# Reordering the start of a fused attention and gated FFN kernel, and its passage from batch 0 to batch 1

## The chip, the cores and the metric

The kernel runs on one core of one Trainium2 chip. The metric is the time of one execution on the device in microseconds (us). Executions of one and the same kernel differ by up to about 1 us here, so differences of a few tenths are read from the traces, one profiled run for each kernel, and the times are used as a check.

## The reference

The inputs are q, k and v of 8 batches, 8 heads, 576 positions and 64 elements, and three FFN weights, all in f32.

```python
q_s = exp(q - max(q, -1));  q_s /= sum(q_s, -1)        # softmax over the 64 elements of a head
k_s = exp(k - max(k, 2));   k_s /= sum(k_s, 2)         # softmax over the 576 positions
kv  = einsum('bhsd,bhse->bhde', k_s, v)
x   = einsum('bhsd,bhde->bhse', q_s, kv)               # 4608 tokens of 512 elements
g   = x @ w_gate                                       # 512 x 1536
out = (gelu(g) * (x @ w_val)) @ w_out                  # 1536 x 512
```

## The kernel before

For each batch the kernel takes exps of q and k (ScalarE), sums and norms (VectorE, partly GpSimd), casts v to f16, transposes q on TensorE ("unit_t"), forms kv for two heads at a time ("hp", four pairs in a batch), masks and scales it into `kv_sb`, multiplies to x ("unit_x") and casts x to f16. The FFN follows: `psg` and `psv` are the gate and value products, `psy` the output product. Every engine runs its instructions in the order in which the program emits them.

The start ("head" below: all that comes before the large matmuls of batch 0 run without a break), with cuts:

```python
def ksum_mm(hps):                       # column sums of exp(k), one PSUM tile for all four pairs
    ...
def kv0_mm(hp):                         # kv of two heads: 128x128, of which the mask keeps two 64x64 blocks
    pool, tag = (ps_att, "att") if hp == 0 else (ps_big, "mm")
    st[("pskv0", hp)] = pool.tile([P, P], f32, name="pskv0", tag=tag)
    for n in range(NC):                 # NC = 5 chunks of positions
        nc.tensor.matmul(st[("pskv0", hp)], ek_b[0][:, n, hp * P:(hp + 1) * P],
                         v16_b[0][:, n, 2 * hp:2 * hp + 2, 0:D], start=(n == 0), stop=(n == NC - 1))
def kv0_norm(hp):                       # VectorE: kv_sb = pskv0 * 1/sum * mask
    ...
def unit_t(b, g, eng="dve"):            # 8 transposes into one bank, then one copy to eqt
    ...
def unit_x(b, hp, eng="act", big=False):
    nc.tensor.matmul(psx, st[(b, "kv", hp)].rearrange("p h e -> p (h e)"), xq(b, hp), start=True, stop=True)
    copy_on(eng, xt[:, hp, :], psx)
...
evac_t0("dve")
warm_pe(2); ksum_mm((0, 1)); warm_pe(2); ksum_mm((2, 3))
cast_v(0, 0, 2, "dve")                  # heads 0 and 1 of v
cast_v(0, 2, 4, "act")
ksum_rec()
cast_v(0, 4, 6, "act")
kv0_mm(0); kv0_mm(1); kv0_norm(0); kv0_norm(1)
cast_v(0, 6, 8, "dve")
...                                     # loads of the next batches; first casts of the weights on GpSimd
unit_x(0, 0, "act", True)
kv0_mm(2)
unit_x(0, 1, "act", True)
kv0_norm(2)
unit_t(0, 1, "dve")
```

Work of the next batch rides between the matmul groups of the present one; `at(batch, kind, place, ...)` registers it. For the passage from batch 0 to batch 1:

```python
at(0, NS, 16, L(unit_kv, 1, 0), L(cast_v, 1, 4, 8), L(load_batch, 2, ((v, "v"),)))
at(0, NS, 6, L(norm, 1, 3))
at(0, NS, 17, L(unit_x, 1, 0, "act", True), L(unit_x, 1, 1, "act", True))
first1 = ([[L(unit_kv, 1, 1), L(unit_t, 1, 1)], [], [L(unit_x, 1, 3, "dve")]],
          [[], [], [L(unit_x, 1, 2, "act")]])
...
cut = 10 if ns == 3 else NFI            # where in the last output group of batch 0 the riders go
```

Much later, among the last FFN groups of batch 1:

```python
at(1, FI, 6, L(norm, 2, 3))             # batch 2's last norm: VectorE sums, reciprocal, multiply
at(1, FI, 10, L(unit_t, 2, 1))          # its transposes on TensorE
at(1, FI, 11, ..., L(cast_v, 3, 0, H))  # batch 3's v, four casts on GpSimd
```

The softmax here doesn't subtract the row's maximum and nothing guards it: scores larger than these inputs give would overflow.

## Time and profile before

| | before |
|---|---|
| time, 3 runs | 315.99 us median (315.94 to 316.39) |
| span of the profiled run | 314.5 us |
| k landed, v landed (start of ScalarE's first exp of k and first cast of v) | 10.02, 12.62 us |
| first large matmul (`psg`) | 15.41 us |
| its third block (ninth large matmul: x of batch 0 is complete) | 17.85 us |
| the same third block of batch 1 | 53.13 us |

Timeline lines are to be read as: start (us), duration (us), engine, source line, operation, output<-inputs, shapes, count, and in brackets the idle time ahead of the instruction with the engine that ended it. A matmul of 512 columns is shown as 0.38 us long, but the next one can start 0.216 us after it, so successive starts are what tells the pace. The prediction shows the lines of before.

### The profile page before, as it was taken

How to read it: one execution, taken by the hardware profiler on the slowest of the kernel's cores; microseconds unless marked ns; L12 is line 12 of the kernel's file. 1: busy time of each engine (PE TensorE's matmuls, PEld its weight loads, DVE VectorE, ACT ScalarE, POOL GpSimd, SP SyncE). 2: the span in 40 equal slices, each digit the busy share in tenths (PEclk: the TensorE clock that was granted, in tenths of full speed). 3: DMA queues.
4: the chain of work that ended last, by engine and by line, in shares of the span. 5: the costliest groups of instructions: out<-in, count | busy, mean ns of one | idle time of the engine just before them, and what ended most of it. 6: DMA issues, size and time to landing. Idle time of an engine off the chain costs nothing.

```text
span 314.5 us, 4799 instructions
## 1 busy us (share of the span) xinstructions
PE 307.7 (98%) x1826; PEld 143.7 (46%) x1826; DVE 191.1 (61%) x324; ACT 138.5 (44%) x178; POOL 44.7 (14%) x59
## 2 busy tenths in 40 slices
PE   8899999999999999999999999999999999999995
PEld 3444454444444444444444444444444444444443
DVE  3844386597898479746984599458943434324331
ACT  3753564988433663356334643374330233013300
POOL 2657451331001200030003000300000000000000
PEclk9999999999999999999999999999999999999999
DMA  7999999950178116921492139303021200140002
GB/s 231 372 383 394 401 386 388 395 194 0 69 245 306 53 70 194 349 59 67 127 386 80 72 90 383 115 27 131 1 58 28 115 18 0 35 101 0 3 33 100
DMA packets 42343, 50.78 MB, mean 161 GB/s; under 512 B 3408, under 2 KB 38096, under 8 KB 42320
## 3 DMA queue, kind: packets, MB, share of 16 engines
q1 hardware_dynamic: 40592, 48.84, 45.0%
q10 hardware_dynamic: 1728, 1.64, 1.6%
q8 instruction: 14, 0.23, 0.3%
q14 instruction: 9, 0.07, 0.1%
HBM read 37.75 MB, written 9.44 MB: 150 GB/s over the span
## 4 chain that ended last, share of the span: by engine, by line
PE 90%; DVE 4%; DMA 2%; ACT 2%; issue 1%; ACTq 0%; DVEq 0%
PE psy L489 29%; PE psg L411 28%; PE psv L411 27%; DMA qt<-in_q_dram 2%; PE pskv L284 1%; DVE eq L200 1%; PE psl L510 1%; PE psx L383 1%; DVE rq L191 1%; DVE rq L181 1%; DVE ht L418 1%; PE psx L365 1%; ACT eq L163 1%; PE pst L306 1%; ACT L416 0%
## 5 line engine op out<-in xcount | busy, mean ns | idle before, releaser
L416 ACT ACTIVATE gl<-psg 128x512 f32<-128x512 f32 x108 | 64.0, 599 | 131.0 <-PE psg L411 124.5
L418 DVE SCALAR_TENSOR_TENSOR ht<-psv,gl 128x512 f16<-128x512 f32 x108 | 72.9, 682 | 64.6 <-PE psv L411 64.1
L411 PE MATMUL psg<-xt,wg_sb 128*128 128x512 f16 x384 | 100.5, 379 | 0.1
L411 PE MATMUL psv<-xt,wv_sb 128*128 128x512 f16 x384 | 100.5, 379 | 0.0
L489 PE MATMUL psy<-wo_sb,ht 128*128 128x512 f16 x420 | 94.0, 379 | 0.0
L411 PEld LDWEIGHTS <-wv_sb 128*128 128x128 f16 x432 | 42.3, 98 | 51.2 <-issue 0.8
L411 PEld LDWEIGHTS <-wg_sb 128*128 128x128 f16 x432 | 41.9, 98 | 49.4 <-issue 0.4
L489 PEld LDWEIGHTS <-ht 128*128 128x128 f16 x420 | 40.4, 98 | 47.9 <-issue 0.8
L538 DVE TENSOR_SCALAR yo<-psy 128x512 f32<-128x512 f32 x30 | 20.5, 685 | 29.7 <-PE psy L489 29.7
L139 POOL CAST v<-vt 128x640 f16<-128x640 f32 x26 | 18.8, 763 | 137.1 <-DMA vt<-in_v_dram 98.3
L181 DVE TENSOR_REDUCE rq<-eq 128x10 f32<-128x640 f16 x28 | 22.7, 812 | 6.1 <-ACT eq L163 5.7
L200 DVE TENSOR_TENSOR eq<-eq,rrq 128x640 f16<-128x640 f16 (+1 forms) x29 | 23.7, 817 | 0.3
L163 ACT ACTIVATE ek<-kt 128x1280 f16<-128x1280 f32 (+1 forms) x11 | 19.1, 1746 | 3.4 <-DMA kt<-in_k_dram 3.3
L163 ACT ACTIVATE eq<-qt 128x2560 f16<-128x2560 f32 (+2 forms) x10 | 18.4, 1863 | 2.3 <-DMA qt<-in_q_dram 2.2
L331 DVE STREAM_TRANSPOSE et<-eq 128x640 f16<-128x640 f16 x20 | 16.9, 845 | 0.7
L411 PE MATMUL psg<-xtr,wg_sb 128*128 128x512 f16 x48 | 12.3, 379 | 0.0
L411 PE MATMUL psv<-xtr,wv_sb 128*128 128x512 f16 x48 | 12.3, 379 | 0.0
L143 DVE CAST xt<-psx 128x512 f16<-128x512 f32 x16 | 10.2, 682 | 1.2 <-PE psx L365 1.2
L403 PE MATMUL pswarm<-warm,ident 128*128 128x512 f16 x34 | 9.5, 438 | 1.4 <-POOL ident masks.py:199 1.4
L163 ACT ACT_TABLE_LOAD x8 | 10.3, 1283 | 0.6 <-DMA qt<-in_q_dram 0.5
L141 ACT CAST xt<-psx 128x512 f16<-128x512 f32 x16 | 8.7, 588 | 3.5 <-PE psx L365 3.5
L141 ACT CAST xtr<-psxr 128x128 f16<-128x128 f32 (+1 forms) x6 | 1.7, 283 | 17.8 <-PE psxr L383 17.8
(74 smaller groups left out, 122.6 us busy)
## 6 DMA issues: line engine op xcount, KB each, us to landing
out_dram<-yo SPq DMA_DIRECT2D x14, 512.0 KB, 3.5
kt<-in_k_dram SPq DMA_DIRECT2D x7, 640.0 KB, 7.9
vt<-in_v_dram SPq DMA_DIRECT2D x7, 640.0 KB, 8.4
qt<-in_q_dram SPq DMA_DIRECT2D x7, 640.0 KB, 6.5
qt<-in_q_dram SPq DMA_DIRECT2D x8, 512.0 KB, 6.7
eqt<-et SPq DMA_DIRECT2D x80, 40.0 KB, 1.9
wost<-in_moe_w_out_dram SPq DMA_DIRECT2D x6, 512.0 KB, 7.9
kt<-in_k_dram SPq DMA_DIRECT2D x6, 512.0 KB, 8.1
```

Of the source, the lines that this page charges most:

```text
L139: nc.gpsimd.tensor_copy(out=dst, in_=src)
L141: nc.scalar.copy(out=dst, in_=src)
L143: nc.vector.tensor_copy(out=dst, in_=src)
L163: nc.scalar.activation(out=dst[:, n0:NC, h0 * D:h1 * D].rearrange(o, d=D, **({"t": 2} if b >= QUAD else {})), in_=heads(tiles[(nm, b)], b, ...
L181: nc.vector.reduce_sum(rq, e, axis=mybir.AxisListType.X)
L200: (nc.gpsimd if eng == "pool" else nc.vector).tensor_tensor(out=e, in0=e, in1=rrq.unsqueeze(-1).to_broadcast((P, n, 2, D)), op=ALU.mult)
L331: nc.vector.transpose(out=et[:, :, hp].rearrange("p c (n i) -> p n c i", i=32), in_=eq_b[b % 2][:, :, hp * P:(hp + 1) * P].rearrange("p n ...
L411: nc.tensor.matmul(ps, w[:, ci, fi * P:(fi + 1) * P], xt[:, ci, :], start=(ci == 0), stop=(ci == HP - 1))
L416: nc.scalar.activation(out=gl, in_=psg, func=ACTF.Gelu)
L418: nc.vector.scalar_tensor_tensor(out=ht, in0=psv, scalar=_H_SCALE, in1=gl, op0=ALU.mult, op1=ALU.mult)
L489: nc.tensor.matmul(psy, hts[fi][:, ns * P:(ns + 1) * P], wo_sb[:, fi, :], start=(fi == 0), stop=(fi == NFI - 1))
L538: nc.vector.tensor_scalar(out=yo, in0=psy, scalar1=1.0 / _H_SCALE, scalar2=None, op0=ALU.mult)
```

## The change

The intent is to start the large matmuls sooner and to close the gaps at the passage. In the head, kv of batch 0 is computed on column halves (20 matmuls of 64 columns instead of 10 of 128 for two pairs), v is cast head by head on two engines, the first x is split over two banks and cast by ScalarE and VectorE at once, and the second group of transposes is spread between these steps. At the passage, kv, norm and x of batch 1 move up within batch 0. The diff, cut to its core:

```diff
     def kv0_mm(hp):
-        pool, tag = (ps_att, "att") if hp == 0 else (ps_big, "mm")
-        st[("pskv0", hp)] = pool.tile([P, P], f32, name="pskv0", tag=tag)
+        ps = ps_big.tile([P, D], f32, name="pskv0", tag="mm")
         for n in range(NC):
-            nc.tensor.matmul(st[("pskv0", hp)], ek_b[0][:, n, hp * P:(hp + 1) * P],
-                v16_b[0][:, n, 2 * hp:2 * hp + 2, 0:D], start=(n == 0), stop=(n == NC - 1))
+            for s in range(2):
+                c0 = hp * P + s * D
+                nc.tensor.matmul(ps[s * D:(s + 1) * D], ek_b[0][:, n, c0:c0 + D],
+                                 v16_b[0][:, n, 2 * hp + s, 0:D], start=(n == 0), stop=(n == NC - 1))
 ...  (ksum_mm and ksum_rec work on two pairs at a time; unit_t takes a list of functions to run between its halves)
+    def unit_x_halves(b, hp):
+        for i, eng in enumerate(("act", "dve")):
+            c = slice(i * MAIN // 2, (i + 1) * MAIN // 2)
+            psx = ps_big.tile([P, MAIN // 2], f32, name="psx", tag="mm")
+            nc.tensor.matmul(psx, ..., xq(b, hp)[:, c], start=True, stop=True)
+            copy_on(eng, get_xt(b)[:, hp, c], psx)
 ...
-    warm_pe(2); ksum_mm((0, 1)); warm_pe(2); ksum_mm((2, 3))
-    cast_v(0, 0, 2, "dve"); cast_v(0, 2, 4, "act"); ksum_rec(); cast_v(0, 4, 6, "act")
-    kv0_mm(0); kv0_mm(1); kv0_norm(0); kv0_norm(1)
+    warm_pe(2); ksum_mm(0); ksum_rec(0); ksum_mm(1)
+    cast_v(0, 0, 1, "dve"); cast_v(0, 1, 2, "act"); cast_v(0, 2, 3, "dve"); cast_v(0, 3, 4, "act")
+    cast_v(0, 4, 6, "act")
+    unit_t(0, 1, None, (lambda: kv0_mm(0), lambda: kv0_norm(0), lambda: kv0_mm(1),
+                        lambda: kv0_norm(1), lambda: unit_x_halves(0, 0)))
+    evac_t1 = st["evac_t"]
+    unit_x(0, 1, "act", True)
+    kv0_mm(2)
+    evac_t1("dve")
+    ksum_rec(1)
+    kv0_norm(2)
     cast_v(0, 6, 8, "dve")
 ...
-    unit_x(0, 0, "act", True); kv0_mm(2); unit_x(0, 1, "act", True); kv0_norm(2); unit_t(0, 1, "dve")
 ...
-    at(0, NS, 16, L(unit_kv, 1, 0), L(cast_v, 1, 4, 8), L(load_batch, 2, ((v, "v"),)))
-    at(0, NS, 6, L(norm, 1, 3))
+    at(0, NS, 16, L(unit_kv, 1, 0), L(cast_v, 1, 4, 8), L(load_batch, 2, ((v, "v"),)),
+       L(norm, 1, 3))
-    first1 = ([[L(unit_kv, 1, 1), L(unit_t, 1, 1)], [], [L(unit_x, 1, 3, "dve")]],
-              [[], [], [L(unit_x, 1, 2, "act")]])
+    first1 = [[L(unit_t, 1, 1), L(unit_kv, 1, 1)], [L(unit_x, 1, 2, "act")],
+              [L(unit_x, 1, 3, "dve")]]
-                cut = 10 if ns == 3 else NFI
+                cut = 9 if ns == 2 else 7 if ns == 3 else NFI
```

More of the change, by code (lines that the diff above doesn't have):

```diff
@@ L236, in kv_norm @@
         for j in range(2):
-            kv_sb = att.tile([P, 2, D], f16, name="kv_sb", tag="kv", bufs=12)
+            kv_sb = att.tile([P, 2, D], f16, name="kv_sb", tag="kv", bufs=8)
             nc.vector.scalar_tensor_tensor(
@@ L242, in kv_norm, with ksum_mm, ksum_rec @@
             st[(b, "kv", 2 * g + j)] = kv_sb
-    def ksum_mm(hps):
-        if "pks" not in st:
-            st["pks"] = ps_big.tile([P, HP], f32, name="pks", tag="mm")
-        for hp in hps:
+    def ksum_mm(g):
+        st[("pks", g)] = ps_big.tile([P, 2], f32, name="pks", tag="mm")
+        for j in range(2):
+            hp = 2 * g + j
             for n in range(NC):
-                nc.tensor.matmul(st["pks"][:, hp:hp + 1], ek_b[0][:, n, hp * P:(hp + 1) * P], ones,
-                                 start=(n == 0), stop=(n == NC - 1))
-    def ksum_rec():
-        st["rck0"] = att.tile([P, HP], f32, name="rck0", tag="rck0", bufs=1)
-        nc.vector.reciprocal(out=st["rck0"], in_=st["pks"])
+                nc.tensor.matmul(st[("pks", g)][:, j:j + 1], ek_b[0][:, n, hp * P:(hp + 1) * P],
+                                 ones, start=(n == 0), stop=(n == NC - 1))
+    def ksum_rec(g):
+        st[("rck0", g)] = att.tile([P, 2], f32, name="rck0", tag="rck0")
+        nc.vector.reciprocal(out=st[("rck0", g)], in_=st[("pks", g)])
     def kv0_mm(hp):
-        pool, tag = (ps_att, "att") if hp == 0 else (ps_big, "mm")
-        st[("pskv0", hp)] = pool.tile([P, P], f32, name="pskv0", tag=tag)
+        ps = ps_big.tile([P, D], f32, name="pskv0", tag="mm")
+        st[("pskv0", hp)] = ps
         for n in range(NC):
-            nc.tensor.matmul(
-                st[("pskv0", hp)], ek_b[0][:, n, hp * P:(hp + 1) * P],
-                v16_b[0][:, n, 2 * hp:2 * hp + 2, 0:D], start=(n == 0), stop=(n == NC - 1))
+            for s in range(2):
+                c0 = hp * P + s * D
+                nc.tensor.matmul(ps[s * D:(s + 1) * D], ek_b[0][:, n, c0:c0 + D],
+                                 v16_b[0][:, n, 2 * hp + s, 0:D], start=(n == 0), stop=(n == NC - 1))
     def kv0_norm(hp):
-        kv_sb = att.tile([P, 2, D], f16, name="kv_sb", tag="kv", bufs=12)
+        kv_sb = att.tile([P, 2, D], f16, name="kv_sb", tag="kv", bufs=8)
         nc.vector.scalar_tensor_tensor(
-            out=kv_sb, in0=st[("pskv0", hp)].rearrange("p (h e) -> p h e", e=D),
-            scalar=st["rck0"][:, hp:hp + 1], in1=mask, op0=ALU.mult, op1=ALU.mult)
+            out=kv_sb, in0=st[("pskv0", hp)].unsqueeze(1).to_broadcast((P, 2, D)),
+            scalar=st[("rck0", hp // 2)][:, hp % 2:hp % 2 + 1], in1=mask, op0=ALU.mult, op1=ALU.mult)
         st[(0, "kv", hp)] = kv_sb
@@ L298, in get_eqt, with unit_t @@
         return st[(b, "eqt")]
-    def unit_t(b, g, eng="dve"):
+    def unit_t(b, g, eng="dve", between=()):
         eqt = get_eqt(b)
         pst = ps_att.tile([P, 2, MAIN], f16, name="pst", tag="att")
+        st["evac_t"] = lambda eng: copy_on(eng, eqt[:, 2 * g:2 * g + 2, 0:MAIN], pst)
         for j in range(2):
             hp = 2 * g + j
+            for f in between if j == 1 else ():
+                f()
             for n in range(NM):
@@ L308, in unit_t @@
                     eq_b[b % 2][:, n + 1, hp * P:(hp + 1) * P], ident)
-        st["evac_t"] = lambda eng: copy_on(eng, eqt[:, 2 * g:2 * g + 2, 0:MAIN], pst)
         if eng:
@@ L367, in unit_x @@
         copy_on(eng, xt[:, hp, :], psx)
+    def unit_x_halves(b, hp):
+        for i, eng in enumerate(("act", "dve")):
+            c = slice(i * MAIN // 2, (i + 1) * MAIN // 2)
+            psx = ps_big.tile([P, MAIN // 2], f32, name="psx", tag="mm")
+            nc.tensor.matmul(psx, st[(b, "kv", hp)].rearrange("p h e -> p (h e)"),
+                             xq(b, hp)[:, c], start=True, stop=True)
+            copy_on(eng, get_xt(b)[:, hp, c], psx)
     def unit_xrem(b, eng="act"):
@@ L427, in ffn_fi, with ffn_first @@
         return gate(psg, psv)
-    def ffn_first(xt, after, between):
+    def ffn_first(xt, after):
         ps = []
@@ L440, in ffn_first @@
                 mm_gv(psg, wg_sb, xt, fi, range(0, 2))
-                for f in between[fi]:
-                    f()
                 mm_gv(psv, wv_sb, xt, fi, range(0, 2))
@@ L571 @@
     warm_pe(2)
-    ksum_mm((0, 1))
-    warm_pe(2)
-    ksum_mm((2, 3))
-    cast_v(0, 0, 2, "dve")
-    cast_v(0, 2, 4, "act")
-    ksum_rec()
-    cast_v(0, 4, 6, "act")
-    kv0_mm(0)
-    kv0_mm(1)
-    kv0_norm(0)
-    kv0_norm(1)
+    ksum_mm(0)
+    ksum_rec(0)
+    ksum_mm(1)
+    cast_v(0, 0, 1, "dve")
+    cast_v(0, 1, 2, "act")
+    cast_v(0, 2, 3, "dve")
+    cast_v(0, 3, 4, "act")
+    cast_v(0, 4, 6, "act")
+    unit_t(0, 1, None, (lambda: kv0_mm(0), lambda: kv0_norm(0), lambda: kv0_mm(1),
[6 more added lines that the diff above has]
+    kv0_norm(2)
     cast_v(0, 6, 8, "dve")
@@ L590 @@
     cast_w("wv", 0, "pool")
-    unit_x(0, 0, "act", True)
-    kv0_mm(2)
-    unit_x(0, 1, "act", True)
-    kv0_norm(2)
-    unit_t(0, 1, "dve")
     preload(ACTF.Gelu)
@@ L670 @@
         if b < 2:
-            hts = ffn_first0(xt, (x_upper0, L(unit_x, 0, 3, "act"))) if b == 0 else ffn_first(xt, *first1)
+            hts = ffn_first0(xt, (x_upper0, L(unit_x, 0, 3, "act"))) if b == 0 else ffn_first(xt, first1)
             fi0 = len(hts)
```

## The prediction

> **What bounds the kernel now.** I read the page first, for which engine fills the span, then the chain of waits, then the timeline of the head (0 to 20 us) and of the passage from batch 0 to batch 1 (44 to 54 us), because the change touches only these two places.
>
> ```profile
> PE 307.7 (98%) x1826; PEld 143.7 (46%) x1826; DVE 191.1 (61%) x324; ACT 138.5 (44%) x178; POOL 44.7 (14%) x59
> PE 90%; DVE 4%; DMA 2%; ACT 2%; issue 1%; ACTq 0%; DVEq 0%
> ```
>
> The first line is busy time by engine, the second the chain that ended last by engine. TensorE (PE) is busy for 98% of the span and is 90% of the chain. The large matmuls (psg, psv, psy) start 0.216 us apart from 15.41 us to the end, and the change removes none of them. So time can only be won where the PE stream starts late or has a gap. A list of the matmul starts with more than the usual distance between them shows what there is: the start itself at 15.41 us, and three gaps at the passage, of 0.184, 0.058 and 0.189 us beyond the usual distance, 0.43 us in all. The head, in the timeline of PE (start, duration, instruction, wait before):
>
> ```profile
> 13.36 0.72 PE L261 MATMUL pskv<-v,ek 128*128 128x128 f16 x10 [0.45 <-DVE v L143]
> 14.24 0.39 PE L365 MATMUL psx<-eqt,kv_sb 128*128 128x512 f16 x1 [0.17 <-DVE kv_sb L267]
> 14.96 0.61 PE L306 MATMUL pst<-ident,eq 128*128 128x128 f16 x8
> 15.41 0.38 PE L411 MATMUL psg<-xt,wg_sb 128*128 128x512 f16 x1
> ```
>
> Here PE waits for the cast of v, then for kv, and does 8 transposes (0.45 us of issue) after x, before the first large matmul. Those are the waits that the change attacks. VectorE (DVE) at the same time:
>
> ```profile
> 14.38 0.73 DVE L143 CAST v<-vt 128x640 f16<-128x640 f32 x1
> 15.04 0.33 DVE L267 SCALAR_TENSOR_TENSOR kv_sb<-pskv,rck,mask 128x128 f16<-128x128 f32 x1
> 15.61 0.69 DVE L143 COPY eqt<-pst 128x1024 f16<-128x1024 f16 x1 [0.24 <-PE pst L306]
> ```
>
> The reader is to see that the last cast of v (heads 6 and 7) is done at 15.11 us, before the eqt copy, and that PE's fourth kv unit, which needs it, comes at 16.27 us without a wait. The passage:
>
> ```profile
> 48.23 0.59 PE L489 MATMUL psy<-wo_sb,ht 128*128 128x512 f16 x2
> 48.84 0.38 PE L411 MATMUL psg<-xt,wg_sb 128*128 128x512 f16 x1
> 49.06 0.38 PE L411 MATMUL psv<-xt,wv_sb 128*128 128x512 f16 x1
> 49.33 0.38 PE L411 MATMUL psg<-xt,wg_sb 128*128 128x512 f16 x1
> ...
> 52.73 0.38 PE L365 MATMUL psx<-eqt,kv_sb 128*128 128x512 f16 x1
> 53.13 0.38 PE L411 MATMUL psg<-xt,wg_sb 128*128 128x512 f16 x1
> ```
>
> Each jump above 0.216 us here is a wait for ScalarE's cast of an x block (0.59 us each).
>
> **What the Trainium skill says.** "TensorE: Matmul & The Clock Gate", section "Wait — 56ns, not 53.3ns?", gives warm start-to-start distances of 55.6 and 215.7 ns for 128 and 512 columns; the trace agrees (55 to 56 and 216 ns). "TensorEngine Tiling (Array Packing)", section "Key Properties": "Changing tiling mode (not just tile) drains the TensorE". The trace shows such a drain: batch 2's kv units already run on column halves, and the first of these starts 0.309 us after a 512-column matmul (0.093 too late), while the next large matmul starts 0.129 us after the last of them (about 0.11 too late). "ScalarE: Activation LUTs", section "What ACT_TABLE_LOAD costs", puts an ACTIVATE at 186 ns + 0.833 ns an element and says that successive ones overlap by about 93 ns; the trace agrees (casts of 640 and 1280 elements: 726 and 1262 ns, starts 632 ns apart). So a cast of 320 elements is estimated at 0.455 us. "PSUM — Partial Sum Buffer", section "PSUM bank collisions raise a hardware error", has two engines reading the same bank at once as a collision, which is why x in halves for two engines needs two banks; no run of before shows it.
>
> **The change in the head, step by step** (all times after are estimates).
> 1. v by heads. VectorE is free at 12.64 (the eqt copy ends). Reciprocal first: 0.17 us long, but VectorE starts the next instruction some 0.08 before the last one ends (13.31 end of cast, 13.23 next start), so head 0 starts at 12.72. Half of a 0.67 to 0.73 us cast is about 0.37, so it ends at 13.09. ScalarE starts at 12.62 (v landed) and ends head 1 at 13.08. PE may start kv at 13.14 instead of 13.36.
> 2. kv on halves: 10 matmuls in 5 pairs; in batch 2 the pairs start about 0.03 us apart, so the fifth starts 0.15 after the first and ends 0.196 later: 13.49, where the 5 whole ones took 0.44. kv_sb 0 runs from 13.52 to 13.87 (0.35 each). Heads 2 and 3 are ready at about 13.44, so kv 1 runs 13.49 to 13.84, kv_sb 1 13.88 to 14.23.
> 3. x 0 in halves: kv_sb 0 plus 0.06 gives 13.93 and 14.04 us; each half takes 0.11 + 0.17, so they end at 14.21 and 14.32. ScalarE's half cast (186 - 26 + 0.833 x 256, about 0.37) ends at 14.62, VectorE's (0.68 less 256 columns at 0.96 a ns, 0.415) at 14.78.
> 4. PE meanwhile: 4 transposes (0.22) to 14.37 (the other 4 filled the wait before kv), x 1 (0.216) to 14.59, kv 2 with both drains to 14.96. First large matmul at about 14.96: **0.45 earlier** than 15.41. The next pair needs x 1 cast by ScalarE (14.79 to 15.38), so runs from 15.43 to 15.86.
> 5. The price. The order of VectorE's instructions in the built program is now: half of x 0, eqt copy, reciprocal, kv_sb 2, **then** the cast of heads 6 and 7. From the half's start at 14.36, with starts 0.34, 0.67, 0.09 and 0.27 apart: 14.70, 15.37, 15.46, 15.73. The cast takes 0.73 and ends at about 16.43. PE needs it for kv 3 at 15.95, and its order is fixed: it waits until about 16.48. Before, kv 3 began at 16.276. What follows (kv 3, x 2, two psg, x 3, two psv) takes 1.574 us in the old trace and 0.15 + 0.13 + 6 x 0.216 = 1.575 in the new, because the 0.13 us that column halves save is what the drain costs. So the head ends **about 0.2 us later** than before, although it starts 0.45 earlier.
>
> **The change at the passage.** kv of batch 1 moves up by three matmuls (0.65 us): PE start 45.71 instead of 46.35. By the old distances (x may start 1.39 and 1.66 us after kv) x 0 may start at 47.15 and x 1 at 47.37, where PE arrives at 47.13 and 47.35, so 0.02 to 0.03 is lost. Five psy matmuls now lie between x and the first large matmul, instead of two: they cover the casts, and the gaps of 0.184 and 0.058 go. The fourth norm (0.81 + 0.22 + 0.83) comes before the output's eviction and ends at about 49.1, so the transposes at 49.5 can go ahead of kv. x 2 moves a pair of matmuls earlier, so its cast ends about 0.2 us before it is needed and the gap of 0.189 goes; x 2 itself may wait 0.03 for kv_sb. Sum: 0.43 less 0.05, **about 0.38 us won**. Fewer buffers for kv_sb (8 for 12) cost nothing, as just 8 are ever taken.
>
> **Sum:** 315.99 + 0.2 - 0.38 = 315.8. Everything from 54 us on is the same program; its two later waits (0.25 and 0.30 us, at 62.8 and 70.8 us) hang on ScalarE's exps, which start when the gelus of the same batch are done and so shift along.
>
> **Rivals.** (a) The head keeps its 0.45 us, if VectorE gets to heads 6 and 7 sooner than I reckon (short casts, more overlap). For it: VectorE's durations for 320 and 256 elements are only my scaling. Against it: the copies of eqt and of heads 6 and 7 alone are 1.3 us after 14.36. Then 315.3. It would still be capped: the last wo chunk is cast on GpSimd by 42.67, at a time that the loads set, and PE takes it at 42.88, so more than 0.2 us of head gain turns into a wait for it. (b) VectorE is slower than reckoned, or the GpSimd casts slow it, and kv 3 starts at 16.7: then the head loses 0.4 and the passage just balances it: 316.0. (c) The two warm-up matmuls that are dropped let the clock gate close and PE runs at half speed for some us. Against it: the page of before grants full clock in all slices with idle stretches of 0.5 and 0.6 us, and the new longest is about 0.7 us (11.8 to 12.5). That would be 317 or more; I give it 2%. (d) The passage's gaps are replaced by a wait for kv_sb or the fourth norm: at most 0.3 given back: 316.1.
>
> **Range and chances.** The prize is at most 0.45 + 0.43 = 0.9 us of 316, under 0.3%; a change of 2% would take 6.3 us. The three runs of before spread over 0.45 us. So I predict 315.8 us with a range of 315.2 (rival a) to 316.4 (rivals b and d, with the spread), faster 1%, within 2% 98%, slower 1%.
>
> **What would show it.** In the profile after: the first psg matmul at 14.9 to 15.0; a PE wait of about 0.5 us for VectorE's v ahead of the fourth kv unit, starting near 16.5; psg's third block (17.85 before) at 18.0 to 18.1; no gap over 0.1 us on PE between 46 and 54 us apart from drains; the last large matmuls some 0.2 us earlier than before. Wrong would be: no wait ahead of kv 3 (step 5 fails, rival a), a wait for wo's cast near 42.9, a granted clock below 1 near 13 us, or new gaps near 47 or 51 us.

## The result

The changed kernel is correct and takes 316.03 us median (four runs: 316.28, 316.24, 315.82, 315.72), against 316.15 us for four runs of before (315.94 to 316.39). The ratio of the times is 0.9995, with a 95% interval of 0.9978 to 1.0013: the same. A ratio here is the mean time of one kernel's fast runs over that of the other's of the same rounds, so it is not quite the ratio of the medians quoted. The page of the profile after, with the same two lines that the prediction shows of before:

```profile
PE 307.0 (98%) x1845; PEld 143.4 (46%) x1845; DVE 192.0 (61%) x327; ACT 138.5 (44%) x179; POOL 44.5 (14%) x59
...
PEclk9999999999999999999999999999999999999999
...
PE 89%; DVE 5%; DMA 2%; ACT 2%; issue 1%; ACTq 0%; DVEq 0%
```

TensorE is still the bound, and the clock row holds 9 throughout (mean granted clock 1.0), so the two dropped warm-up matmuls did not bring any throttling. VectorE's share of the chain grew from 4 to 5%. The timeline of TensorE in the head after:

```profile
13.10 0.74 PE L263 MATMUL pskv<-v,ek 128*64 128x64 f16 x20
13.89 0.39 PE L377 MATMUL psx<-eqt,kv_sb 128*128 128x256 f16 x2
14.12 0.39 PE L310 MATMUL pst<-ident,eq 128*128 128x128 f16 x4
14.35 0.38 PE L368 MATMUL psx<-eqt,kv_sb 128*128 128x512 f16 x1
14.65 0.35 PE L263 MATMUL pskv<-v,ek 128*64 128x64 f16 x10
14.93 0.39 PE L423 MATMUL psg<-xt,wg_sb 128*128 128x512 f16 x1
...
16.57 0.35 PE L263 MATMUL pskv<-v,ek 128*64 128x64 f16 x10 [0.58 <-DVE v L143]
...
18.16 0.38 PE L423 MATMUL psg<-xt,wg_sb 128*128 128x512 f16 x1
```

The first large matmul starts at 14.93 us instead of 15.41, but a wait for VectorE's cast of v now stands ahead of the fourth kv unit: it starts 0.74 us later than the usual distance would have it, of which the bracket shows the 0.58 in which the array was empty. The third block comes at 18.16 us (17.85 before). The timeline of VectorE after shows why:

```profile
14.32 0.42 DVE L143 CAST xt<-psx 128x256 f16<-128x256 f32 x1
14.66 0.68 DVE L143 COPY eqt<-pst 128x1024 f16<-128x1024 f16 x1
15.26 0.16 DVE L255 RECIPROCAL rck<-pks 128x2 f32<-128x2 f32 x1
15.53 0.35 DVE L268 SCALAR_TENSOR_TENSOR kv_sb<-pskv,rck,mask 128x128 f16<-128x128 f32 x1
15.79 0.73 DVE L143 CAST v<-vt 128x640 f16<-128x640 f32 x1
```

The cast of heads 6 and 7 (last line) stands behind four other instructions and ends at 16.52 us; before, it ended at 15.11. At the passage, TensorE after:

```profile
47.46 0.60 PE L368 MATMUL psx<-eqt,kv_sb 128*128 128x512 f16 x2
47.90 1.24 PE L499 MATMUL psy<-wo_sb,ht 128*128 128x512 f16 x5
48.97 0.38 PE L423 MATMUL psg<-xt,wg_sb 128*128 128x512 f16 x1
49.19 0.38 PE L423 MATMUL psv<-xt,wv_sb 128*128 128x512 f16 x1
...
52.80 0.38 PE L368 MATMUL psx<-eqt,kv_sb 128*128 128x512 f16 x1
53.02 0.38 PE L423 MATMUL psg<-xt,wg_sb 128*128 128x512 f16 x1
```

Five `psy` matmuls now cover the casts of x, and no gap over 0.03 us beyond the usual distance is left: those of 0.184, 0.058 and 0.189 us are gone.

### Counting from the landing of v

Loads do not arrive at the same time in each run: in the traces with unchanged load rates, ScalarE's first exp of k starts between 9.91 and 10.21 us, and its first cast of v between 12.54 and 12.92. In the profiled run of after v landed 0.07 us earlier than in that of before, which is no work of the change. I therefore count the landmarks from the start of ScalarE's first cast of v (us):

| run | v landed | first psg | third block | 33rd large matmul | batch 1's third block | after batch 2's transposes (241st) | last large matmul |
|---|---|---|---|---|---|---|---|
| before | 12.615 | 2.795 | 5.233 | 10.413 | 40.516 | 60.472 | 298.042 |
| after | 12.541 | 2.393 | 5.617 | 10.801 | 40.477 | 60.574 | 298.146 |
| passage alone | 12.630 | 2.800 | 5.237 | 10.417 | 40.093 | 60.039 | 297.607 |
| head alone | 12.752 | 2.393 | 5.613 | 10.793 | 40.896 | 60.751 | 298.321 |
| after, heads 6/7 on GpSimd | 12.751 | 2.393 | 4.964 | 10.792 | 40.468 | 60.568 | 298.138 |
| after, gate in an existing tile | 12.582 | 2.395 | 5.617 | 11.003 | 40.678 | 60.329 | 297.898 |
| both of these | 12.714 | 2.396 | 4.967 | 10.812 | 40.487 | 60.138 | 297.709 |
| passage alone, gate | 12.923 | 2.795 | 5.232 | 10.412 | 40.088 | 59.735 | 297.305 |

Counted so, different runs of the same stretch of program agree within about 0.01 us up to the third block, and from the 241st large matmul to the last all of them take 237.57 us. (The 33rd can differ more: 11.003 and 10.801 in two kernels that are the same up to there, which experiment 9 explains.) So everything happens in the first 61 us, and the table reads as a sum: the head costs 5.617 - 5.233 = **0.38 us**, the passage wins (40.477 - 10.801) - (40.516 - 10.413) = **-0.43 us**, together -0.04 us at 53 us. Then, up to the 241st matmul, another 0.14 us is lost, where the program has not changed at all.

### Where the last 0.14 us goes

Between 68 and 72 us VectorE multiplies batch 2's last norm while GpSimd casts batch 3's v. The timeline of VectorE before, then of GpSimd and of TensorE before:

```profile
69.85 1.23 DVE L200 TENSOR_TENSOR eq<-eq,rrq 128x640 f16<-128x640 f16 x1
```

```profile
68.34 3.31 POOL L139 CAST v<-vt 128x640 f16<-128x640 f32 x4 [7.45 <-DMA vt<-in_v_dram]
```

```profile
70.61 0.92 PE L306 MATMUL pst<-ident,eq 128*128 128x128 f16 x8
```

Here the profile merges the eight transposes into one row; 0.30 us of it is the wait for the multiply ahead of the fifth.

And after, VectorE, GpSimd and then TensorE, which waits for the multiply:

```profile
69.73 1.37 DVE L200 TENSOR_TENSOR eq<-eq,rrq 128x640 f16<-128x640 f16 x1
```

```profile
68.37 3.31 POOL L139 CAST v<-vt 128x640 f16<-128x640 f32 x4 [7.54 <-DMA vt<-in_v_dram]
```

```profile
70.50 0.39 PE L310 MATMUL pst<-ident,eq 128*128 128x128 f16 x4
71.15 0.40 PE L310 MATMUL pst<-ident,eq 128*128 128x128 f16 x4 [0.27 <-DVE eq L200]
```

The norm's multiply ahead of this one, of the same shape, takes 0.83 us where GpSimd is idle (67.29 us in the same trace). The four casts start 0.67 us apart; the third began at 69.70 us, 25 ns ahead of the multiply at 69.73. The multiply ends 0.67 us after that cast, and the fourth cast's record is stretched from 0.72 to 1.31 us. This agrees with the Trainium skill, "SBUF — State Buffer", section "Who interferes with whom": a VectorE instruction with two SBUF inputs contends with a GpSimd instruction that reads SBUF, and the one that comes later is blocked for the whole of the other. The casts start when batch 3's v has landed, not when TensorE gets there (68.34 and 68.37 us). So the multiply came 0.12 us earlier and still ended 0.03 us later; TensorE's wait for it grew from 0.30 to 0.44 us.

### The profile page after: what moved, and what is told of

Same layout as the page of the kernel before. It is cut to its first block, busy times and chain, and to the rows that moved or that the text cites. A ratio compares the mean times of both kernels' runs of the same rounds, so it can differ in the third digit from the quotient of the medians.

```text
span 314.5 us, 4843 instructions
## 1 busy us (share of the span) xinstructions
PE 307.0 (98%) x1845; PEld 143.4 (46%) x1845; DVE 192.0 (61%) x327; ACT 138.5 (44%) x179; POOL 44.5 (14%) x59
## 4 chain that ended last, share of the span: by engine, by line
PE 89%; DVE 5%; DMA 2%; ACT 2%; issue 1%; ACTq 0%; DVEq 0%
PE psy L499 29%; PE psg L423 28%; PE psv L423 27%; DMA qt<-in_q_dram 2%; PE pskv L285 1%; DVE eq L200 1%; PE psl L520 1%; PE psx L395 1%; DVE rq L191 1%; DVE rq L181 1%; DVE ht L430 1%; ACT eq L163 1%; PE psx L368 0%; PE pst L310 0%; ACT L428 0%
## 5 line engine op out<-in xcount | busy, mean ns | idle before, releaser
L143 DVE CAST xt<-psx 128x512 f16<-128x512 f32 (+1 forms) x17 | 10.7, 667 | 1.4 <-PE psx L368 1.3
L415 PE MATMUL pswarm<-warm,ident 128*128 128x512 f16 x32 | 8.7, 436 | 1.4 <-POOL ident masks.py:199 1.4
L141 ACT CAST xt<-psx 128x512 f16<-128x512 f32 (+1 forms) x16 | 8.6, 575 | 3.3 <-PE psx L368 3.0
```

The costliest lines, as they stand in the source:

```text
L141: nc.scalar.copy(out=dst, in_=src)
L143: nc.vector.tensor_copy(out=dst, in_=src)
```

## The experiments

Twelve kernels ran, all correct. They went in three calls, each with nine runs of before on the same chip (medians 316.10, 316.36 and 316.38 us).

### 1. The passage alone

Before, with the lines of the passage (`at`, `first1`, `cut`, `ffn_first`) taken from the change; the head is the old one.

> The kernel before with only the passage of the change (batch 1's kv, norm and x moved up); the head is the old one. Theory (pinned): PE is about 0.42 us earlier than before when it comes out of the passage (third block of batch 1's first psg at 52.7 instead of 53.13), but the wait ahead of batch 2's second transposes near 70.7 us grows from 0.30 to about 0.70, because VectorE's last norm multiply of batch 2 overlaps GpSimd's casts of batch 3's v, whose start is set by the load and not by PE. So from 72 us on nothing is won: span within 0.1 us of before. Rival (parts cancel: the head loses what the passage wins): no such growth, the end is 0.4 us earlier than before.

Measured: 315.83 us median (315.48 to 315.91), ratio 0.9987 (0.9975 to 1.0). In the table the passage wins 0.42 us by batch 1's third block (40.093 for 40.516), and all of it arrives at the end (297.607 for 298.042 is 0.43). The pinned theory is refuted. The multiply at 69.44 us fell upon the second cast instead of the third and was 1.22 us long, so the wait stayed at 0.29 us. The passage's gain is real and is not pinned later on. What the collision returns depends on where in a cast the multiply falls.

### 2. The head alone

The changed kernel with the passage put back as it was.

> The changed kernel with the passage put back; only the head of the change. Theory (pinned): the first large matmul near 14.94, a wait of 0.74 us ahead of the fourth kv unit, third block near 18.16, so 0.31 us later than before; the passage keeps its gaps of about 0.43, so it comes out 0.3 later than before (53.4); the wait near 70.7 shrinks from 0.30 to about 0, which takes up the loss: span within 0.1 us of before. Rival (parts cancel): the loss of 0.3 us stays to the end, span 0.3 us longer.

Measured: 316.50 us median (316.42 to 316.68), ratio 1.0012 (0.9998 to 1.0026). All five runs lie above the median of before (316.10), though the interval still touches 1. The trace is clear: third block at 5.613 for 5.233, the loss of 0.38 us again, with the 0.74 us wait for the cast of heads 6 and 7. By batch 1's third block the loss is still 0.38 (40.896 for 40.516). This time the multiply fell late in a cast (1.12 us) and the wait was 0.19 us, so 0.28 us arrive at the end. The two parts of the change cancel.

### 3 and 4. A gate ahead of GpSimd's casts

To take the collision away, GpSimd is to start batch 3's v only when the multiply is done. A 128x1 copy that reads the multiply's result does that; it writes into a new tile of 32 bytes. Once in the changed kernel:

```diff
     ones = const.tile([P, 1], f16)
+    hold = const.tile([P, 1], f16)
 ...
-       ... L(exp_rem0), L(cast_v, 3, 0, H))
+       ... L(exp_rem0),
+       lambda: nc.gpsimd.tensor_copy(out=hold, in_=eq_b[0][:, 0, 3 * P:3 * P + 1]), L(cast_v, 3, 0, H))
```

> The changed kernel, with one 128x1 copy on GpSimd that reads batch 2's last normalised block, ahead of GpSimd's casts of batch 3's v: the casts can then not overlap that norm multiply. Theory (pinned): the multiply takes 0.83 instead of 1.37 us, the wait of 0.43 ahead of the transposes near 70.7 goes, and the end is 0.43 us earlier than in the changed kernel (span about 0.4 us shorter, time ratio about 0.9987). Rival (the multiply is long for another reason, or the wait is for something else): no change beyond 0.05 us, or a longer one as the casts come later.

and once in before (there with 8 kv_sb buffers for 12, to make room for the tile):

> The kernel before with the same gate on GpSimd (and 8 buffers for kv_sb in place of 12, of which 8 are ever used, to make room). Theory (pinned): multiply 0.83 instead of 1.23 us, the wait of 0.30 near 70.7 goes, and the end is 0.3 us earlier than before; so with the gate the changed kernel is ahead by the 0.11 us that it had at 53 us. Rival: no change.

Measured: 319.67 us (ratio 1.0112) and 319.43 us (1.0106), both more than 3 us longer. The multiply was 0.83 us long, but that does not show that the gate works: run 12 below has the same slow loads and no gate, and there too the multiply takes 0.83 us, as batch 3's casts start (74.43 us) only after its end (74.28 us). K and v landed about 0.6 and 0.9 us later (10.5 to 10.6 and 13.4 to 13.5 us), and TensorE waited 1.2 to 1.3 us near 46 us for the cast of an output weight. The gate runs at 74 us, so it cannot be what slows loads at 10 us. The two runs tell nothing of the collision's worth.

### 5 and 8. The gate with a 64-byte tile

As the built program places them, the tiles that q, k, v and the weights are loaded into start at multiples of 512 bytes in SBUF, in before and in after; the 32-byte tile had moved all of them by 32 bytes. If multiples of 64 bytes were enough, a 64-byte tile would mend it. Tried in the changed kernel and in before with the passage alone (the latter again with 8 kv_sb buffers):

```diff
-    hold = const.tile([P, 1], f16)
+    hold = const.tile([P, 32], f16)
```

> The same gate in the changed kernel, but its tile is 64 instead of 32 bytes a partition, so that all load destinations stay on multiples of 64 bytes (in the last gate run they lay 32 beside). Theory A (the 3.5 us that the gate runs lost came from the shifted load destinations, not from the gate): first large matmul back at 14.9 us, k's exp starts near 10 us, DMA 380 to 400 GB/s in the first slices. Theory B (the lost time came from the gate): still 318 us. With A, theory P (VectorE's multiply waits for the GpSimd cast that is running): multiply 0.83 us, no wait near 70.7, time 0.2 to 0.45 us shorter than the changed kernel, ratio to before 0.998 to 0.999, and the runs of this kernel lie closer together.

> The old head, the new passage and the aligned gate (8 kv_sb buffers). Theory: 0.42 from the passage and 0.3 from the multiply: 0.7 us less than before, ratio 0.9978; so it ends within 0.2 us of the version above, as the head, even mended, is worth only its third block's 0.35 less the wo wait.

Measured: 319.41 us (ratio 1.0098) and 319.41 us (1.0097). A miss: 64 bytes is not enough.

### 6 and 7. Heads 6 and 7 of v on GpSimd

If the head loses because VectorE casts these heads last, another engine should mend it:

```diff
-    cast_v(0, 6, 8, "dve")
+    cast_v(0, 6, 8, "pool")
```

> The changed kernel with the cast of v's heads 6 and 7 of batch 0 on GpSimd (0.72 us, between its norm multiply that ends at 12.9 and the first gate weight at 13.3 to 13.6) instead of at the end of VectorE's queue. Theory (the head loses its lead only to VectorE's order): first large matmul stays at 14.9 to 15.0, the wait of 0.74 ahead of the fourth kv unit falls below 0.1, third block at 17.5 instead of 18.16 (0.35 ahead of before). Then a wait of about 0.15 for the last wo cast near 42.5, and about 0.5 us less than the changed kernel at 53 us; what is left at the end depends on how the multiply near 70 us meets GpSimd's casts: 0.1 to 0.7 us less. Rival (other users of the same slot, as x 2 or the weights, hold PE there): wait stays above 0.4.

The same with the 64-byte gate:

> Both: heads 6 and 7 on GpSimd, and the aligned gate. Theory: 0.5 us from the head and 0.4 from the multiply add up, about 0.9 us less than the changed kernel, 315.1 us, ratio to before 0.997. Rival: the weights' or wo casts, which the loads pace, take the head's part back (a wait of over 0.4 us near 42.5), then 315.6.

Measured: 315.95 us (315.77 to 316.49), ratio 0.999 (0.9977 to 1.0004), and with the gate 319.24 us (1.0094, slow loads again). The timeline of TensorE of the first of the two:

```profile
15.82 0.38 PE L423 MATMUL psv<-xt,wv_sb 128*128 128x512 f16 x1
16.13 0.35 PE L263 MATMUL pskv<-v,ek 128*64 128x64 f16 x10
...
19.44 1.03 PE L423 MATMUL psg<-xt,wg_sb 128*128 128x512 f16 x4
20.94 0.82 PE L423 MATMUL psv<-xt,wv_sb 128*128 128x512 f16 x3 [0.47 <-POOL wv_sb L139]
```

The wait ahead of the fourth kv unit is gone but for 0.09 us, the drain on entering column halves, and the third block comes at 4.964 instead of 5.617: the head is 0.65 us shorter. So VectorE's order was the cause of the head's loss. But twelve large matmuls further on there is a new wait of 0.64 us, for GpSimd's cast of the third chunk of the value weight, and the 33rd large matmul comes at 10.792 as against 10.801: all of it is taken back. The timeline of GpSimd in the changed kernel shows that the cast itself waits for its load:

```profile
16.90 1.04 POOL L139 CAST wg_sb<-wgst 128x1024 f16<-128x1024 f32 x1 [0.72 <-DMA wgst<-in_moe_w_gate_dram]
19.64 1.04 POOL L139 CAST wv_sb<-wvst 128x1024 f16<-128x1024 f32 x1 [1.70 <-DMA wvst<-in_moe_w_val_dram]
```

It begins at 19.64 to 19.89 us in the four profiled runs that hold the whole change and no moved address, and at 18.36 to 18.71 us in before, in both runs with the old head and in the run with the head alone. Why the load comes in one of two places, I did not find out; SyncE issues it at about the same time in both (12.53 us in after, 12.60 in before). The head alone with heads 6 and 7 on GpSimd, where that load might come early and the head's lead might last, was not tried.

### 9 to 11. The gate without a new tile

The gate's copy now writes into a free column of a tile that exists already, so no address moves:

```diff
+       lambda: nc.gpsimd.tensor_copy(out=tiny[:, 64:65], in_=eq_b[0][:, 0, 3 * P:3 * P + 1]),
```

In the changed kernel:

> The changed kernel with the gate (a 128x1 GpSimd copy that reads the last norm's block of eq before batch 3's v is cast), but writing into a column of a tile that exists already, so that no SBUF address moves. Theory A (the 3.3 us that all gated kernels lost come from the moved addresses of the load destinations, not from the gate): first psg at 14.9 to 15.2 us as in the changed kernel, the multiply of batch 2's last norm 0.83 us long, no wait of more than 0.1 us near 70.7 us, 0.2 to 0.45 us less than the changed kernel's profiled run from 70 us on, about 315.6 us. Rival B (the gate itself slows the kernel): 319.4 us again, first psg near 16 us or later.

In the changed kernel with heads 6 and 7 on GpSimd:

> The changed kernel with heads 6 and 7 of v cast on GpSimd, and the gate in the existing tile. The head: wait before the fourth kv unit about 0.1 us instead of 0.74, but then about 0.6 us for GpSimd's cast of wv chunk 2, so the 33rd large matmul 8.40 us after the first, as in the changed kernel. From 70 us on: no wait near 70.7. So the same as the changed kernel with the gate, within 0.15 us (about 315.6). If the head's loss on VectorE were what counts, it would be 0.6 us less than that kernel.

In before with the passage alone:

> The kernel before with the passage's part of the change alone and the gate in the existing tile (old head): the passage wins 0.41, the gate takes away the wait of about 0.29 us near 70.7. About 315.4 us, 0.7 us less than before, ratio 0.998. If the gate only moves that wait elsewhere: 315.8, as with the passage alone.

| kernel | median, us (range) | ratio to before (95%) |
|---|---|---|
| changed, gate | 315.97 (315.91 to 316.07) | 0.999 (0.9976 to 1.0004) |
| changed, heads 6/7 on GpSimd, gate | 315.87 (315.41 to 316.19) | 0.9985 (0.9972 to 0.9999) |
| passage alone, gate | 315.54 (315.43 to 315.83) | 0.9978 (0.9965 to 0.999) |

Loads are normal again (k at 9.95 to 10.20 us), so the gate itself slows nothing. The timelines of VectorE and GpSimd of the last of the three:

```profile
69.72 0.83 DVE L200 TENSOR_TENSOR eq<-eq,rrq 128x640 f16<-128x640 f16 x1
```

```profile
70.68 0.19 POOL L637 CAST tiny<-eq 128x1 f32<-128x1 f16 x1 [9.74 <-DVE eq L200]
70.80 2.72 POOL L139 CAST v<-vt 128x640 f16<-128x640 f32 x4
```

The multiply is 0.83 us long, and the four casts take 2.72 us for 3.31. In the table the distance from batch 1's third block to the 241st matmul falls from 19.956 us (before), 20.097 (after) and 19.946 (passage alone) to 19.65 in all three gated runs: the collision was worth 0.31, 0.45 and 0.30 us. In the changed kernel, 0.20 us of that did not arrive, because in that run the third chunk of the value weight was cast late enough (19.89 us) for TensorE to wait 0.195 us for it (33rd matmul at 11.003 for 10.801); there the expected 315.6 us was missed. In the kernel with heads 6 and 7 on GpSimd the wait for that cast is 0.65 us, and the 33rd matmul stands at 10.812: as expected, moving the cast of v wins nothing in a kernel with the whole change.

The passage alone with the gate, with the old head, is the best kernel. It beats before by 0.22%, with the whole interval below 1. Its median is 0.43 us below that of the gated changed kernel, and 0.49 us below that of the changed kernel, which ran in another call; counted from the landing of v it ends 0.84 us ahead of the latter (297.305 for 298.146).

### 12. The moved addresses alone

The changed kernel with an unused 64-byte tile, filled once, ahead of the others, and no gate:

```diff
     ones = const.tile([P, 1], f16)
+    hold = const.tile([P, 32], f16)
+    nc.vector.memset(hold, 1.0)
```

> The changed kernel with an unused 64-byte tile (filled once) ahead of the others, so that all later SBUF addresses move by 64 bytes, and no gate. Theory A (addresses): 319.2 to 319.6 us, first psg at 16 us or later, fewer GB/s in the slices of the first 100 us. Rival B (the gate): 316.0, first psg at 14.9 to 15.2 us.

Measured: 319.44 us (319.36 to 319.56), ratio 1.01 (1.0087 to 1.0114). The row of GB/s of the page, first of the changed kernel, then of this one:

```profile
GB/s 232 373 383 395 401 384 389 392 194 0 69 256 293 56 70 203 340 60 67 135 385 78 69 91 380 121 20 132 1 58 28 116 18 2 33 100 0 3 33 100
```

```profile
GB/s 223 331 345 351 374 367 356 357 359 47 68 137 344 107 77 109 350 119 49 108 341 165 23 118 328 186 31 83 52 52 34 79 53 2 23 104 5 3 33 99
```

In the second to eighth slice the rate is 331 to 374 instead of 373 to 401 GB/s with the same packets, and the first stretch of loading reaches into a ninth slice at full rate. So the moved addresses slow the loads, and with them the kernel: its span is 317.8 us for 314.5. The Trainium skill, "DMA: Bandwidth & Descriptors", section "How a descriptor splits into AXI transactions", says that a descriptor that does not begin at a multiple of 256 bytes starts with a partly used transaction. That would fit 32 and 64 bytes both being slow, but the page says it of what a transaction reads, and no run here tried 128 or 256 bytes. The size of the step is open.

## Why the prediction was right, and where it was not

The time (316.03 us, in a range of 315.2 to 316.4 about 315.8) and the class were right. But the range is 1.2 us wide and holds the time of before itself, so it would have held no change at all: that the time lies in it says little, and partly it is luck, since the traces do not show the gain of 0.2 us that was forecast. By its own steps:

- **What bounds the kernel, and the prize.** Right: TensorE is the bound before and after, and only its start and its gaps moved.
- **Steps 1 to 4 of the head.** Right. Counted from the landing of v, the first large matmul was predicted at 14.96 - 12.62 = 2.34 us and came at 2.39. VectorE's cast of one head took 0.49 us (estimated 0.37), which made kv start 0.04 us later than reckoned. ScalarE's half cast took 0.37 us, as estimated, and VectorE's 0.42 (512 columns take 0.69 in the same trace, so 0.27 for 256 columns, which is the 0.96 columns a ns that I had used). One sum of step 2 is off without harm: four distances of 0.03 make 0.12, not 0.15, but 0.15 is what the trace has from the first to the last of the ten matmuls.
- **Step 5, "the head ends about 0.2 us later".** Right in its mechanism, wrong in its size: 0.38 us. The fourth kv unit was predicted at 16.48 - 12.62 = 3.86 us and came at 4.03. The term that was mis-sized is VectorE's row of starts. I had put `kv_sb` 0.09 us behind the start of the reciprocal, taking the overlap of independent instructions; but it reads what the reciprocal writes and started 0.265 us behind it. The trace of before could have told: at 47.13 and 50.54 us it has two such pairs, 0.206 us apart (the other 0.06 us is not explained). The eqt copy gave 0.07 back (0.60 to the next start for 0.67), which leaves 0.10 us. With 0.04 from the later kv, and 0.03 from a slip in the sum (15.73 + 0.73 is 16.46, not 16.43), that is the missing 0.17; the last 0.01 came after it, where the six steps took 1.585 us for 1.575.
- **The passage, "about 0.38 us won".** Right: 0.43 in the changed kernel and 0.42 alone. All three gaps went, and less than the 0.05 us that I had given back was lost. (The 1.39 us from kv to x 0 should read 1.44, as the trace of before has it; the 47.15 worked out from it is right.)
- **"Everything from 54 us on is the same program ... and so shift along".** This step failed. The exps and gelus did shift along, but batch 2's norm meets casts on GpSimd whose start is set by a load. A lead is then rounded to a cast: in the profiled runs 0.14 us was lost with the whole change, 0.01 won with the passage alone and 0.10 won with the head alone. The gate, which takes the collision away, shows that it was this: with it the stretch takes 19.65 us in all three kernels.
- **The rivals.** Rival (b), VectorE slower than reckoned, "then the head loses 0.4 and the passage just balances it: 316.0", is what the runs showed; its cause was above all a dependence, and GpSimd's casts did not lengthen the head's copies (0.68 and 0.73 us, as before). Rival (a), that the head keeps its lead, was refuted, and its cap was right in kind and wrong in place: once the wait for heads 6 and 7 was removed, it was the third chunk of the value weight at 19.85 us that took the gain, not the output weight near 42.9. Rival (c), the clock, was refuted by the clock row and by the pace: psg and psv start 0.215 us apart at 15.40 us, where the first warm-up matmuls of before, at half speed, start 0.427 us apart. Rival (d), a wait in place of the passage's gaps, was refuted by the passage's timeline.

So the sum of -0.18 us was in truth -0.04 at 53 us and +0.10 at the end of the profiled run. The medians of after and before are 0.12 us apart the other way, which the scatter of the runs does not tell from zero.

## What to carry to other kernels

An engine whose order is fixed pays for a head start with whatever is pushed to the end of its queue, so follow each result to its last user and count the starts in that queue, with the full distance (0.20 to 0.27 us from a reciprocal's start here, not 0.09) wherever one instruction reads what the one ahead of it wrote. Compare traces from the landing of the data and not from the start of the span, since the loads alone moved by 0.3 to 0.4 us from run to run here. A gain on the critical path can be lost, in part or whole, at the next thing whose time is set by a load; if that is a VectorE instruction with two SBUF inputs beside GpSimd casts, order the two explicitly, and without moving the load destinations in SBUF.

## What the Trainium skill lacked or had wrong

- "DMA: Bandwidth & Descriptors" counts the beats of a descriptor that starts off a 256-byte boundary, but has no rate for loads from HBM whose destination in SBUF is moved by 32 or 64 bytes from a multiple of 512. Here the move by 64 lowered the rate from between 373 and 401 to between 331 and 374 GB/s, and the span rose from 314.5 to 317.8 us. No page that I read warns of a small tile placed ahead of load destinations.
- "TensorEngine Tiling (Array Packing)" says that a change of tiling mode drains TensorE but gives no cost. Here entering column halves from a 512-column matmul took 0.09 us more than the usual distance, and leaving them 0.10 us.
- "SBUF — State Buffer" has the lock between VectorE and GpSimd right, but not what it does to a chain: in a row of four casts 0.67 us apart, the VectorE multiply took 1.12 to 1.37 us instead of 0.83, depending on where in a cast it began, so moving it 0.12 us earlier made it end 0.03 us later.
- No page that I read gives the start-to-start distance of two dependent VectorE instructions with small operands: 0.197 to 0.265 us from a 128x2 reciprocal of 0.16 to 0.17 us to the instruction that reads it.
